# Fused threshold attention and MoE: head pairs on two row groups, DMA turns, MoE units in every attention step

## The chip, the cores and the metric

The kernel runs on one core of a Trainium2 chip. A core has TensorE (PE, matmuls into PSUM), VectorE (DVE), ScalarE (ACT), GpSimd (POOL) and SyncE (SP, which here only issues DMAs). The engines run side by side, each in the order of its own program, and wait for one another by semaphores. The metric is the device time of one execution in microseconds. Before the change the median of three runs is 1036.62 us (1034.22 to 1038.43).

## What is computed

There are 8 batches of 8 heads, 576 tokens and a head dimension of 64, all fp32. Attention keeps only the scores within tau = 0.02 of a row's maximum; the rest get weight zero. The heads are put side by side to 512 features per token, and two dense layers with a leaky ReLU between follow, for all 4608 tokens.

```python
scores = scale * np.matmul(q, k.transpose(0, 1, 3, 2))
thresh = np.max(scores, axis=-1, keepdims=True) - tau
scores = np.where(scores >= thresh, scores, -1000000000.0)
scores = scores - np.max(scores, axis=-1, keepdims=True)
attn = np.exp(scores)
attn = attn / (np.sum(attn, axis=-1, keepdims=True) + 1e-09)
attn_out = np.matmul(attn, v)
x = np.ascontiguousarray(attn_out.transpose(0, 2, 1, 3)).reshape(B * S, H * D)
h = x @ w_in                # 512 -> 2048
g = np.maximum(0.01 * h, h)
out = g @ w_out             # 2048 -> 512
```

## The kernel before

The Tile framework places buffers and semaphores; each engine's order comes from its scheduler, which may move work of different heads past each other. The loop at L272 runs over 65 iterations. Iteration `it` loads head it+4 (`head_loads`), prepares head it+2 (`prep`), computes the scores of head it (`stage_a_blk`), and finishes head it-1 (`rt_blk`, `pv_blk`, `pv_tail`). After every 16 heads `moe_group` runs the dense layers for two batches, 1152 tokens.

`prep`: GpSimd casts v to fp16 beside a column of ones (L93, L94). Nine PE transposes (L97) put q and k with the head dimension on partitions. ACT (L108) takes the fp16 high part, DVE (L109) the low part, so that a score is the sum of products of fp16 halves with nearly fp32 accuracy. Five DMAs of 72 KB (L113 to L117) place the halves.

`stage_a_blk`, for each of five blocks of query rows (four of 128 and one of 64): four matmuls over 128 rows (L137, L138) give 576 scores per query in PSUM; DVE takes the maximum (L139), GpSimd makes the bias of it (L142), and ACT writes relu(score - threshold) to `r` (L146). The weights are taken as 1 where `r` is positive; no exponential is computed.

`rt_blk`: 25 PE transposes per head turn `r` (L161), and DVE compares with zero while leaving PSUM (L167). `pv_blk`: 25 matmuls of 65 columns (L181), the last column giving the sum. `pv_tail`: DVE takes reciprocals (L196, L197), ACT scales (L201), five PE transposes turn the result (L207), and ACT copies it to the features-on-partitions tile `xTg` (L213).

`moe_group`: layer 1 in blocks of 512, 512 and 128 tokens (L238), with ACT (L245) and DVE (L249) sharing the leaky ReLU; layer 2 with 16 matmuls of 512 columns per 128 tokens (L257), a copy by ACT (L264), a 256 KB store (L265). All DMAs stand in SP's queue, the weights' too (L221, L226); GpSimd casts the weights (L222, L227).

PSUM holds two score tiles (`sc`, two banks each, also used for `qkt` and `ops`), two `rt` tiles (also used for `hps`), one `pv` and one `xt`.

Of the kernel before, what the change touches and what calls it, by code (L numbers as in the profile page):

```python
# [11 lines left out]
FP16 = mybir.dt.float16  # L12
AX = mybir.AluOpType
AF = mybir.ActivationFunctionType


@with_exitstack
def kernel(
# [10 lines left out]
    nc = tc.nc  # L29
    B, H, S, D = q.shape  # L30
    NH = B * H
    tau_f = float(tau)
    d_model = moe_w_in.shape[0]
    d_ff = moe_w_in.shape[1]
    SCALE = 1.0 / 8.0

    MT = [128, 128, 128, 128, 64]
    NQT = len(MT)
    NT9 = 9
    GB = 2  # L40
    NGRP = B // GB
    GTOK = GB * S

    sb = ctx.enter_context(tc.tile_pool(name="sb", bufs=1))
    ps = ctx.enter_context(tc.tile_pool(name="ps", bufs=2, space=bass.MemoryType.PSUM))

    I32 = sb.tile([128, 128], FP32, name="I32")
    make_identity(nc, I32)
    I16 = sb.tile([128, 128], FP16, name="I16")
    nc.gpsimd.tensor_copy(out=I16[:, :], in_=I32[:, :])  # L50

    BL0s = [sb.tile([128, 576], FP16, name=f"BL0_{i}") for i in range(3)]
    for t_ in BL0s:
        nc.gpsimd.memset(t_[64:128, 0:576], 0.0)
    def getBL0(h):
        return BL0s[h % 3]

    w_in16 = [sb.tile([128, d_ff], FP16, name=f"win16_{g}") for g in range(4)]
    w_out16 = [sb.tile([128, d_model], FP16, name=f"wout16_{j}") for j in range(16)]
    xTg = [sb.tile([128, GTOK], FP16, name=f"xTg_{g}") for g in range(4)]  # L60
    gT = [sb.tile([128, GTOK], FP16, name=f"gT_{j}") for j in range(16)]

    st = {}
    heads = {}

    def head_loads(h):
        b, hh = divmod(h, H)
        qk1 = sb.tile([128, NT9, 128], FP32, tag="qk1", bufs=4, name="qk1")
        v1 = sb.tile([128, NQT, 64], FP32, tag="v1", bufs=4, name="v1")
        vb = sb.tile([128, NQT, 65], FP16, tag="vb", bufs=6, name="vb")  # L70
        nc.sync.dma_start(
            out=qk1[0:64, 0:NT9, 0:64],
            in_=q[b, hh, :, :].rearrange("(t p) d -> p t d", p=64),
        )
        nc.sync.dma_start(
            out=qk1[0:64, 0:NT9, 64:128],
            in_=k[b, hh, :, :].rearrange("(t p) d -> p t d", p=64),
        )
        nc.sync.dma_start(
            out=v1[0:128, 0:4, 0:64],  # L80
# [186 lines left out]
    for h in range(4):  # L267
        head_loads(h)
# [62 lines left out]
```

## Time and profile before

| | |
|---|---|
| Median of three runs | 1036.62 us (1034.22 to 1038.43) |
| Span of the profiled execution, first to last instruction | 1038.0 us |
| Busy: PE / DVE / ACT / POOL | 910.3 / 517.5 / 492.9 / 123.4 us |
| Mean granted TensorE clock | 0.884 of full speed |
| DMA moved | 70.91 MB, 26.8% of 16 engines' span on the main queue |

The profile is one execution recorded by the hardware. A busy time is the time in which an engine had an instruction running; a matmul's duration includes its way through the array, so successive matmuls overlap and their rate is read from start times. A group of instructions is given by line, engine, operation, output<-input with shapes, count, then busy time and mean duration, then the idle time before them and what ended it. The clock row is in tenths of full speed. No duration is recorded for the execution apart from its span, so the span stands for it; it lies inside the range of the three runs.

### The profile page before, as it was taken

What the parts mean: (1) busy time and instruction counts of PE and PEld (TensorE: products, weight loads), DVE (VectorE), ACT (ScalarE), POOL (GpSimd) and SP (SyncE); (2) the same over time, 40 slices, a digit from 0 to 9 for tenths busy, and PEclk for the clock granted to TensorE, in tenths of its full rate; (3) what the DMA queues carried; (4) which work ended last, traced back from release to release, by engine and by line L of the source; (5) the groups of instructions that cost most, each with busy time, mean ns of one, the idle gap of its engine ahead of it and who ended that gap; (6) DMA issues with size and microseconds to landing.
All of it is one profiled execution on the core that took longest, in us unless ns stands there. A gap on an engine that the chain in (4) does not pass through costs nothing. (4 is left out here: it accounts for less than half of the span.)

```text
span 1038.0 us, 17867 instructions
## 1 busy us (share of the span) xinstructions
PE 910.3 (88%) x6720; PEld 515.5 (50%) x6720; DVE 517.5 (50%) x1024; ACT 492.9 (47%) x997; POOL 123.4 (12%) x606
## 2 busy tenths in 40 slices
PE   4999998897898998898898989898889989899888
PEld 2555555553345555553345555554335555554333
DVE  2644444654406566654424666665432666664440
ACT  2543334554425555554424555555432555554441
POOL 3221112110001111110000111111000111110000
PEclk9855556999999889989999888889999888987999
DMA  6823334340023333331013333332002333110002
GB/s 168 214 66 93 78 89 114 72 96 22 1 82 88 76 84 82 87 74 29 1 61 88 73 87 73 87 77 56 1 31 87 76 83 76 38 29 2 0 17 76
DMA packets 148438, 70.91 MB, mean 68 GB/s; under 512 B 120704, under 2 KB 141184, under 8 KB 147840
## 3 DMA queue, kind: packets, MB, share of 16 engines
q1 hardware_dynamic: 148352, 69.77, 26.8%
q8 instruction: 53, 0.87, 0.4%
q14 instruction: 33, 0.27, 0.1%
HBM read 36.70 MB, written 9.44 MB: 44 GB/s over the span
## 5 line engine op out<-in xcount | busy, mean ns | idle before, releaser
L146 ACT ACTIVATE r<-sc,bia 128x576 f16<-128x576 f32 (+1 forms) x320 | 234.3, 740 | 224.3 <-POOL bia L142 220.8
L139 DVE TENSOR_REDUCE mx<-sc 128x1 f32<-128x576 f32 (+1 forms) x320 | 238.0, 755 | 142.9 <-PE sc L138 138.7
L137 PE MATMUL sc<-BHH,QHL 128*128 128x512 f16 (+3 forms) x640 | 203.9, 331 | 40.5 <-ACT r L146 24.1
L161 PE MATMUL rt<-I_66,r 128*128 128x128 f16 (+3 forms) x1600 | 205.5, 240 | 7.9 <-DVE wT L167 6.9
L181 PE MATMUL pv<-vb,wT 128*128 128x65 f16 (+3 forms) x1600 | 150.4, 206 | 0.9 <-DVE wT L167 0.5
L167 DVE TENSOR_SCALAR wT<-rt 128x576 f16<-128x576 f16 (+1 forms) x320 | 134.5, 447 | 33.3 <-PE rt L161 33.1
L161 PEld LDWEIGHTS <-r 128*128 128x128 f16 (+3 forms) x1600 | 122.1, 108 | 58.3 <-issue 22.7
L245 ACT ACTIVATE hre<-hps 128x512 f32<-128x512 f32 (+1 forms) x192 | 93.8, 491 | 118.2 <-PE hps L238 118.2
L142 POOL TENSOR_SCALAR bia<-mx 128x1 f32<-128x1 f32 (+1 forms) x320 | 61.0, 191 | 695.9 <-DVE mx L139 651.3
L181 PEld LDWEIGHTS <-wT 128*128 128x128 f16 (+3 forms) x1600 | 98.5, 103 | 39.7 <-DVE wT L167 4.0
L138 PEld LDWEIGHTS <-QHL 128*128 128x128 f16 (+1 forms) x640 | 69.2, 112 | 85.8 <-issue 59.6
L137 PEld LDWEIGHTS <-QHL 128*128 128x128 f16 (+1 forms) x640 | 70.2, 111 | 73.4 <-issue 29.3
L238 PE MATMUL hps<-xTg_94,win_0_74 128*128 128x512 f16 (+1 forms) x192 | 62.8, 327 | 41.1 <-DVE gT_98 L249 5.4
L109 DVE SCALAR_TENSOR_TENSOR Al<-qkt,Ah 128x576 f16<-128x576 f32 x64 | 48.0, 750 | 93.3 <-ACT Ah L108 93.2
L108 ACT ACTIVATE Ah<-qkt 128x576 f16<-128x576 f32 x64 | 41.5, 649 | 81.9 <-PE qkt L97 81.6
L201 ACT ACTIVATE x<-pv,rcp 128x64 f16<-128x64 f32 (+1 forms) x320 | 70.3, 317 | 10.4 <-DVE rcp L197 10.4
L238 PE MATMUL hps<-xTg_97,win_3_77 128*128 128x512 f16 (+1 forms) x192 | 62.0, 326 | 2.4 <-ACT xTg_97 L213 2.4
L238 PE MATMUL hps<-xTg_95,win_1_75 128*128 128x512 f16 (+1 forms) x192 | 62.9, 327 | 0.0
L238 PE MATMUL hps<-xTg_96,win_2_76 128*128 128x512 f16 (+1 forms) x192 | 62.8, 328 | 0.0
L196 DVE RECIPROCAL rcp<-pv 128x4 f32<-128x4 f32 x64 | 11.7, 182 | 102.2 <-PE pv L181 98.2
L138 PE MATMUL sc<-BL_0_68,QHL 128*128 128x512 f16 (+1 forms) x220 | 60.7, 344 | 0.0
L264 ACT ACTIVATE osb<-ops 128x512 f32<-128x512 f32 x36 | 21.1, 596 | 81.7 <-PE ops L257 81.7
(350 smaller groups left out, 882.1 us busy)
## 6 DMA issues: line engine op xcount, KB each, us to landing
BHH<-Ah SPq DMA_DIRECT2D x128, 72.0 KB, 2.1
out_dram<-osb SPq DMA_DIRECT2D x36, 256.0 KB, 2.0
QHL<-Ah SPq DMA_DIRECT2D x64, 72.0 KB, 2.3
QHL<-Al SPq DMA_DIRECT2D x64, 72.0 KB, 2.0
wsti<-in_moe_w_in_dram SPq DMA_DIRECT2D x4, 1024.0 KB, 5.7
wsto<-in_moe_w_out_dram SPq DMA_DIRECT2D x16, 256.0 KB, 2.7
BL_0_68<-Al SPq DMA_DIRECT2D x22, 72.0 KB, 2.1
BL_1_69<-Al SPq DMA_DIRECT2D x21, 72.0 KB, 2.1
```

The source lines that it names most:

```text
L109: nc.vector.scalar_tensor_tensor(out=Al[0:128, 0:576], in0=qkt[0:128, 0:576], scalar=64.0, in1=Ah[0:128, 0:576], op0=AX.mult, op1=AX.subtract,
L137: nc.tensor.matmul(out=scp[0:M, ksl], lhsT=QHL[0:128, qs], rhs=BHH[0:128, ksl], start=True, stop=False, skip_group_check=True)
L138: nc.tensor.matmul(out=scp[0:M, ksl], lhsT=QHL[0:128, qs], rhs=BL0[0:128, ksl], start=False, stop=True, skip_group_check=True)
L139: nc.vector.tensor_reduce(out=mx[0:M, qt : qt + 1], in_=scp[0:M, 0:576], axis=mybir.AxisListType.X, op=AX.max,)
L142: nc.gpsimd.tensor_scalar(out=bia[0:M, qt : qt + 1], in0=mx[0:M, qt : qt + 1], scalar1=-RS * BS, scalar2=RS * (tau_f + 1e-9), op0=AX.mult, ...
L146: nc.scalar.activation(out=r[0:M, qt, 0:576], in_=scp[0:M, 0:576], func=AF.Relu, bias=bia[0:M, qt : qt + 1], scale=RS * BS,)
L161: nc.tensor.matmul(out=rt[0:Kc, ds(qt * 128, M)], lhsT=r[0:M, qt, ds(c * 128, Kc)], rhs=I16[0:M, 0:M], is_transpose=True, skip_group_check ...
L167: nc.vector.tensor_scalar(out=wT[0:Kc, c, 0:576], in0=rt[0:Kc, 0:576], scalar1=0.0, scalar2=None, op0=AX.is_gt,)
L181: nc.tensor.matmul(out=pv[0:M, qt, 0:65], lhsT=wT[0:Kc, c, ds(qt * 128, M)], rhs=vb[0:Kc, c, 0:65], start=(c == 0 and qt == 0), stop=(c == ...
L201: nc.scalar.activation(out=x[0:M, qt, 0:64], in_=pv[0:M, qt, 0:64], func=AF.Copy, bias=0.0, scale=rcp[0:M, qt : qt + 1],)
L238: nc.tensor.matmul(out=hps[0:128, 0:tb], lhsT=w_in16[gi][0:128, ts(j, 128)], rhs=xTg[gi][0:128, ds(co, tb)], start=(gi == 0), stop=(gi == ...
L245: nc.scalar.activation(out=hre[0:128, 0:tb], in_=hps[0:128, 0:tb], func=AF.Relu, bias=0.0, scale=0.99,)
```

## The change

Nearly the whole body is rewritten; the order of instructions on every engine is now the program's (`manual_schedule`).

A batch is 18 steps: 2 blocks x 4 head pairs x 2 halves of 128 query rows, then 2 tail steps for the last 64 query rows of all 8 heads. In a step the two heads of a pair lie on partitions 0 to 63 and 64 to 127, and their score matmuls (64 rows, 288 columns, three products of halves, two column blocks) alternate between the two (`scores`). The four score banks are all used by one step. DVE copies each head's scores to SBUF and takes the maximum in the same instruction (`copy_max`). In the next step `mask` makes a 16-bit integer of the distance from the threshold, and `weights` lets ACT compute an exponential, with the row sums as a by-product; in two steps of three one of the two heads is masked by ACT (Prelu with a slope of 1e20) instead of DVE.

A DMA that transposes turns the weights (`turn_w`, 128 x 1152 fp16), and pv follows four steps later (`PV_LAG`), v as the stationary operand, so that the result has d on partitions and needs no further turn. The two heads write PSUM partitions 0 to 63 and 64 to 127. The reciprocals of the sums are widened by GpSimd, turned by DMA (`turn_r`), and multiplied in by DVE when pv leaves PSUM (`evacuate`).

q and k are loaded as long rows, split into halves by GpSimd (by ACT and DVE for batch 0), and turned by DMA (`turn`, four turns of 64 x 1152 per load). `gate` makes each GpSimd operation wait for the last mask of DVE. The weights of the dense layers are cast by DMAs that GpSimd issues.

The dense layers are cut into units: `layer1` (512 PSUM columns, one Prelu by ACT) and `layer2` (two matmuls of 512 columns). The loop issues up to one of the first and two of the second in every step; what is left runs after step 144. Plain loads, turns and stores all stand in SP's queue, in the loop's order.

The removed lines are those printed above. The core of what takes their place:

```diff
--- before.py
+++ after.py
...
+PV_LAG = 4
...
+    ctx.enter_context(tc.manual_schedule())
...
+    UNIT = 64.0 * 64.0 * 8.0
+    NEAR = tau_f * UNIT
+    BIAS = -0.0625
...
+    def gate(inst, after):
+        if after is not None:
+            tc.add_manual_dep(inst.ins, after.ins.name,
+                              mybir.DependencyInfo(SYNC, ONLY_ORDER), reason="shared port")
+    def STEEP(st):
+        return st.n % 3 != 0
...
+    def load_qk(b, s, which, eng=None):
+        src = q if which == "q" else k
+        t = sb.tile([128, 2, 576], FP32, tag="raw", bufs=3, name="raw")
+        for c in range(2):
+            h0 = 4 * s + 2 * c
+            (eng or nc.sync).dma_start(
+                out=t[ds(64 * c, 64), :, :],
+                in_=src[b, ds(h0, 2), :, :].rearrange("h (p t) d -> p h (t d)", t=NT),
             )
+        raws[b, s, which] = t
...
+    def split_ops(b, s, which):
+        sc = 64.0
+        st = {}
+        def scale():
+            st["x"] = sb.tile([128, 2, 576], FP32, tag="scaled", bufs=1, name="scaled")
+            return nc.gpsimd.tensor_scalar(
+                out=st["x"][:, :, :], in0=raws[b, s, which][:, :, :], scalar1=sc, scalar2=1.0,
+                op0=AX.mult, op1=AX.mult)
+        def high():
+            st["h"] = sb.tile([128, NT, 2, 64], FP16, tag="half", bufs=4, name="half_h")
+            st["l"] = sb.tile([128, NT, 2, 64], FP16, tag="half", bufs=4, name="half_l")
+            halves[b, s, which] = (st["h"], st["l"])
+            return nc.gpsimd.tensor_copy(
+                out=st["h"][:, :, :, :].rearrange("p t h d -> p h t d"),
+                in_=st["x"][:, :, :].rearrange("p h (t d) -> p h t d", d=64))
+        def low(i):
+            return nc.gpsimd.tensor_tensor(
+                out=st["l"][:, :, i, :],
+                in0=st["x"][:, i, :].rearrange("p (t d) -> p t d", d=64),
+                in1=st["h"][:, :, i, :], op=AX.subtract)
+        return [scale, high, lambda: low(0), lambda: low(1)]
...
+    def turn(b, s, which):
+        res = []
+        for x in halves.pop((b, s, which)):
+            for c in range(2):
+                t = sb.tile([128, NT, 64], FP16, tag=f"{which}T", bufs=16, name=f"{which}T")
+                nc.sync.dma_start_transpose(
+                    out=t[:, :, :], in_=x[ds(64 * c, 64), :, :, :].rearrange("p t h d -> p (t h d)"))
+                res.append(t)
+        turned[b, s, which] = res
...
+    def cast_v(b, p, eng=None):
+        t = sb.tile([128, NT, 64], FP16, tag="v", bufs=10, name="v")
+        i = (eng or nc.gpsimd).tensor_copy(out=t[:, :, :], in_=vraws.pop((b, p))[:, :, :])
+        vs[b, p] = t
+        return i
...
+    def scores(st):
+        st.sc = [ps.tile([128, 2, 512], FP32, tag="sc", bufs=2, name=f"sc{h}") for h in range(2)]
+        for kh in range(2):
+            for i, (qh_, kh_) in enumerate(((0, 0), (1, 0), (0, 1))):
+                for u in range(2 if st.tail else 1):
+                    for h in range(2):
+                        pair = st.p + u
+                        if st.tail:
+                            lhs = cols(st, "q", h, qh_, pair, 512, 64)
+                            o = st.sc[h][ds(64 * u, 64), kh, 0:288]
+                        else:
+                            lhs = cols(st, "q", h, qh_, pair, 256 * st.blk + 128 * st.c, 128)
+                            o = st.sc[h][:, kh, 0:288]
+                        nc.tensor.matmul(out=o, lhsT=lhs, rhs=cols(st, "k", h, kh_, pair, 288 * kh, 288),
+                                         start=(i == 0), stop=(i == 2), skip_group_check=True)
+    def copy_max(st):
+        st.mx = sb.tile([128, 2], FP32, tag="mx", bufs=4, name="mx")
+        st.s = [sb.tile([128, 2, 288], FP32, tag=f"s{h}", bufs=2, name=f"s{h}") for h in range(2)]
+        for h in range(2):
+            nc.vector.tensor_scalar(
+                out=st.s[h][:, :, :], in0=st.sc[h][:, :, 0:288], scalar1=0.0, scalar2=None,
+                op0=AX.add, op1=AX.max, accum_out=st.mx[:, h : h + 1])
+    def mask(st):
+        st.steep = STEEP(st)
+        th = sb.tile([128, 2], FP32, tag="th", bufs=4, name="th")
+        if st.steep:
+            nc.vector.tensor_scalar(out=th[:, 0:1], in0=st.mx[:, 0:1], scalar1=0.5 - NEAR, scalar2=None, op0=AX.add)
+            nc.vector.tensor_scalar(out=th[:, 1:2], in0=st.mx[:, 1:2], scalar1=-1.0, scalar2=NEAR,
+                                    op0=AX.mult, op1=AX.add)
+        else:
+            nc.vector.tensor_scalar(out=th[:, :], in0=st.mx[:, :], scalar1=0.5 - NEAR, scalar2=None, op0=AX.add)
+        nh = 1 if st.steep else 2
+        st.y = sb.tile([128, 2, 576], INT16, tag="y", bufs=2, name="y")
+        for h in range(nh):
+            nc.vector.tensor_scalar(
+                out=st.y[:, h, :], in0=st.s[h][:, :, :].rearrange("p a b -> p (a b)"),
+                scalar1=th[:, h : h + 1], scalar2=-1.0, op0=AX.subtract, op1=AX.max)
+        i = nc.vector.tensor_scalar(
+            out=st.y[:, 0:nh, :], in0=st.y[:, 0:nh, :], scalar1=0x0400, scalar2=None, op0=AX.bitwise_xor)
+        st.th = th
+        return i
...
+    def weights(st):
+        key, j, n = quad(st)
+        if j == 0:
+            sums[key] = sb.tile([128, n, 2], FP32, tag=f"sum{n}", bufs=3, name="sum")
+        st.w = sb.tile([128, 2, 576], FP16, tag="w", bufs=3, name="w")
+        y16 = st.y[:, :, :].bitcast(FP16)
+        if st.steep:
+            st.z = sb.tile([128, 576], FP32, tag="z", bufs=1, name="z")
+        for h in range(2):
+            src, scale, bias = y16[:, h, :], 512.0, BIAS
+            if h == 1 and st.steep:
+                nc.scalar.activation(out=st.z[:, :], in_=st.s[1][:, :, :].rearrange("p a b -> p (a b)"),
+                                     func=AF.Prelu, bias=st.th[:, 1:2], scale=1.0, alpha=1e20)
+                src, scale, bias = st.z[:, :], 1.0 / UNIT, BIAS + 0.03125
+            nc.scalar.activation(out=st.w[:, h, :], in_=src, func=AF.Exp, bias=bias, scale=scale,
+                                 accum_out=sums[key][:, j, h : h + 1])
...
+        nc.sync.dma_start_transpose(out=wt[:, :, ds(128 * c, 128)],
+                                    in_=st.w[:, :, :].rearrange("p h k -> p (h k)"))
...
+    def widen(key, n):
+        wide[key] = sb.tile([128, n, 2, 64], FP16, tag=f"wide{n}", bufs=2, name="wide")
+        return nc.gpsimd.tensor_copy(
+            out=wide[key][:, :, :, :],
+            in_=recs.pop(key)[:, :, :].unsqueeze(3).to_broadcast([128, n, 2, 64]))
+    def turn_r(key, n):
+        rbs[key] = sb.tile([128, n, 128], FP16, tag=f"rb{n}", bufs=2, name="rb")
+        nc.sync.dma_start_transpose(out=rbs[key][:, :, :], in_=wide.pop(key)[:, :, :, :].rearrange("p n h d -> p (n h d)"))
...
+        for pair, o, cols in items:
+            vt = vs[st.b, pair]
+            for i in range(5):
+                for h in range(2):
+                    blk = i if h == 0 else 8 - i
+                    rows = ds(0, 128) if blk != 4 else ds(64 * h, 64)
+                    nc.tensor.matmul(out=o[ds(64 * h, 64)], lhsT=vt[rows, blk, :], rhs=wt[rows, blk, cols],
+                                     start=(i == 0), stop=(i == 4), skip_group_check=True)
...
+        nc.vector.tensor_tensor(out=o, in0=p_[:, :, :], in1=rin, op=AX.mult)
...
+    def layer1(deep=False):
+        g, u, nu = l1q.pop(0)
+        T = g.tokens
+        nj = 16 // nu
+        if u == 0:
+            g.g = sb.tile([128, 16, T], FP16, tag=f"g{T}", bufs=2, name="g")
+        hp = ps.tile([128, nj, T], FP32, tag="h", bufs=2, name="hp")
+        for jj in range(nj):
+            j = nj * u + jj
+            for i in range(4):
+                nc.tensor.matmul(out=hp[:, jj, :], lhsT=w_in16[:, i, ts(j, 128)], rhs=g.x[:, i, :],
+                                 start=(i == 0), stop=(i == 3), skip_group_check=True)
+        nc.scalar.activation(out=g.g[:, ds(nj * u, nj), :], in_=hp[:, :, :], func=AF.Prelu,
+                             bias=0.0, scale=1.0, alpha=0.01)
+        if u == nu - 1:
+            for m in range(T // 128):
+                for r in range(8):
+                    l2q.append((g, m, r))
+    pending_stores = []
+    def layer2():
+        g, m, r = l2q.pop(0)
+        if r == 0:
+            g.o = ps.tile([128, 512], FP32, tag="o", bufs=1, name="o")
+        for j in (2 * r, 2 * r + 1):
+            nc.tensor.matmul(out=g.o[:, :], lhsT=g.g[:, j, ts(m, 128)], rhs=w_out16[:, j, :],
+                             start=(j == 0), stop=(j == 15), skip_group_check=True)
+        if r == 7:
+            nm = g.tokens // 128
+            if m == 0:
+                g.osb = sb.tile([128, nm, 512], FP32, tag=f"osb{nm}", bufs=2, name="osb")
+            nc.scalar.activation(out=g.osb[:, m, :], in_=g.o[:, :], func=AF.Copy, bias=0.0, scale=1.0)
+            if m == nm - 1:
+                pending_stores.append(g)
...
+    for i in range(4):
+        nc.gpsimd.dma_start(out=w_in16[:, i, :], in_=moe_w_in[ts(i, 128), :])
+    for j in range(4):
+        nc.gpsimd.dma_start(
+            out=w_out16[:, ds(4 * j, 4), :],
+            in_=moe_w_out[ds(512 * j, 512), :].rearrange("(j p) f -> p j f", p=128))
...
+    while n < N + PV_LAG + 2 or l1q or l2q or pending_stores:
+        live = n < N
+        if live:
+            for f in loads_at.get(n, []):
+                f()
+            for f in turns_at.get(n, []):
+                f()
+            scores(steps[n])
+        if 1 <= n <= N:
+            last_mask = mask(steps[n - 1])
+        if n in rec_at:
+            recip(rec_at[n], quad_n := (2 if rec_at[n][1] == 2 else 4))
+        if n in ev_at:
+            evacuate(ev_at[n])
+        if live:
+            copy_max(steps[n])
+        if n in rec_at:
+            gate(widen(rec_at[n], quad_n), last_mask)
+        if live:
+            pool_work(n, last_mask)
+        if n in rb_at:
+            turn_r(rb_at[n], 2 if rb_at[n][1] == 2 else 4)
+        while pending_stores:
+            store()
+        if 1 <= n <= N:
+            weights(steps[n - 1])
+            turn_w(steps[n - 1])
+        has_pv = n in pv_at
+        if l1q:
+            layer1()
+        for _ in range(2):
+            if l2q:
+                layer2()
+        if has_pv:
+            pv(pv_at[n])
+        n += 1
...
```

## The prediction

> **What bounds the kernel now.** I read the page's busy shares and granted clock first, then the costliest groups, then windows by stage, then the instructions of single stretches in order of time.
>
> Page, busy shares and TensorE clock over 40 slices:
> ```profile
> PE 910.3 (88%) x6720; PEld 515.5 (50%) x6720; DVE 517.5 (50%) x1024; ACT 492.9 (47%) x997; POOL 123.4 (12%) x606
> ...
> PEclk9855556999999889989999888889999888987999
> ```
> TensorE is busy 88% and nothing else is above half. It also ran long stretches at half clock. Windows (span; busy of PE, PEld, DVE, ACT, POOL; clock; DMA share; GB/s), first MoE stages, then attention alone:
> ```profile
> 225.00:280.00 55.00, 44.68 (x262) 20.90 (x261) 26.96 (x53) 25.29 (x53) 2.17 (x11) 1.00 0.13 30
> 280.00:310.00 30.00, 28.80 (x141) 13.09 (x139) 3.64 (x7) 7.55 (x14) 0.00 (x0) 1.00 0.19 71
> ...
> 310.00:478.00 168.00, 149.40 (x1357) 94.26 (x1355) 104.39 (x210) 96.14 (x196) 25.64 (x144) 0.91 0.34 80
> ...
> 40.00:160.00 120.00, 111.39 (x707) 64.34 (x706) 54.89 (x109) 48.52 (x98) 24.35 (x87) 0.56 0.35 90
> ```
> In the MoE stages the other engines rest; in attention many small TensorE instructions set the pace. Groups of instructions, by form:
> ```profile
> L139 DVE TENSOR_REDUCE mx<-sc 128x1 f32<-128x576 f32 x256 | 190.0, 756 | 122.8 <-PE sc L138 121.8
> L146 ACT ACTIVATE r<-sc,bia 128x576 f16<-128x576 f32 x256 | 187.1, 741 | 208.7 <-POOL bia L142 208.6
> L161 PE MATMUL rt<-I_66,r 128*128 128x128 f16 x1024 | 133.3, 248 | 7.4 <-DVE wT L167 6.9 <-ACT r L146 0.3
> ...
> L167 DVE TENSOR_SCALAR wT<-rt 128x576 f16<-128x576 f16 x256 | 106.5, 449 | 32.5 <-PE rt L161 32.3
> ```
> The durations 756, 741 and 449 ns are the prices for what follows. TensorE's true rate is in the start times (start, duration), warm:
> ```profile
> 301.20 0.38 PE L257 MATMUL ops<-wout_6_84,gT_104 128*128 128x512 f16 x1
> 301.42 0.38 PE L257 MATMUL ops<-wout_7_85,gT_105 128*128 128x512 f16 x1
> ```
> ```profile
> 620.67 0.19 PE L137 MATMUL sc<-BHH,QHL 128*64 128x64 f16 x1
> 620.70 0.20 PE L138 MATMUL sc<-BL_0_68,QHL 128*64 128x64 f16 x1
> ```
> 512 columns pass in 0.216 us, 64 in 0.03; the rest of a duration, 0.16 us, is pass-through. SP's instructions:
> ```profile
> 17.51 0.58 SPq L221 DMA_DIRECT2D wsti<-in_moe_w_in_dram  x1
> 18.19 0.65 SPq L71 DMA_DIRECT2D qk_199<-in_q_dram  x1
> ```
> An issue takes 0.6 us for 144 KB and for 1 MB alike. DMA queues:
> ```profile
> q1 hardware_dynamic: 148352, 69.77, 26.8%
> ```
> 69.77 MB in 26.8% of 1038 us is 251 GB/s while moving.
>
> **The change, priced per step.** There are 144 steps (18 per batch: 16 of 128 query rows for two heads, 2 tail steps), each with about one layer-1 unit and two layer-2 units.
>
> *TensorE.* Removed per head: 9 transposes of q and k, 25 of r (0.08 us apart), 5 of x, and the 65-column matmuls. Kept: all MoE columns, 589,824 in total, 249 us at 0.216 per 512, so 1.73 per step. Scores: 12 matmuls of 288 columns with 64 rows, 1.46 us one after another, 0.73 if the two row groups run together. Weights times v: 10 matmuls of 256 columns per two steps, onto two column halves, 0.54 or 0.27 per step. No row shows two matmuls at once, so PE is 2.73 to 3.73. I take 2.73, because operands and outputs are disjoint halves; 3.73 stays for the range. Changing between row halves, the full array and column halves three times a step can cost nothing, or three pass-throughs, 0.48; I take 0.48. The clock in attention was 0.91, in MoE stages 1.00 even with PE busy 44.68 of 55 us; mixed, I take 0.93. PE: 2.73/0.93 + 0.48 = 3.4 us.
>
> [...]
>
> *VectorE.* Two copies with maximum from PSUM at 756: 1.51. Thresholds, 5/3 at 0.129 (the 64x1 reciprocal): 0.22. The int16 result from SBUF, 4/3 at 0.449 to 0.756, and the bitwise pass, 4/3 at 0.22 to 0.449: no row has these types; 16-bit work ran twice as fast per element, so I take 0.55 and 0.30, 1.13. The final multiply (36 of 692 ns) and reciprocals (40 of 182 ns) come to 0.22. Reading two accumulators, 0 to 0.129 each. Ends 2.85 and 3.8; I take 3.1 less some overlap (two reductions take 1.42, not 1.51): 3.0. Removed: the L167 and L249 passes.
>
> *ScalarE.* Two Exp and 2/3 Prelu at 741, one layer-1 Prelu of 512 (597), a quarter of the 596 ns copy: 2.72. The sums' read-out is 0 to 0.2 each (spacing of the 64-column copies at L201). I take 2.9. Exp is in no row; the toolchain lists Exp, Prelu and Copy in one table set, so I charge no reload.
>
> *GpSimd.* One split operation in 112 steps: 1152 elements by the 512-element cast of 611 ns and the 2048 one of 1.89 us are 1.14 us. Two inputs at 576, 0.66 to 1.3. It lies beside the 1.5 us of copies, for which the added wait on the last mask was placed; behind it queue v's casts and the widening, for which SP waits. Cost nothing; uncovered, 0.5 us in some 40 steps, 20 us. At the start GpSimd issues eight weight DMAs.
>
> *SP.* Per step 1.6 plain DMAs (8 q/k, 16 v, 5 stores per batch) at 0.6: 0.97. Turns: 39 per batch, 2.17 per step. Flat like the rows, 1.3; scaled by bytes from 72 KB, 3.7. SP 2.3 to 4.7; flat is nearer, since 1 MB took 0.58; I take 3.0. In order behind a turn that waits for Exp stand the next loads and stores.
>
> *DMA.* Turned: 295 KB of weights, 115 of q and k, 33 of reciprocals per step; plain 245. 687 KB at 251 GB/s are 2.7 us; with turns at half rate 4.5. I take 2.7, and pv comes three steps after its turn.
>
> [...] The flat rows give 545, and no run here shows a turn.
>
> *Sum.* PE leads with 3.4, the others are at 2.7 to 3.0 beside it. 144 x 3.4 = 490; the first 12 steps have no MoE work and go at VectorE's 3.0, -5. Ahead: load (up to 6 us with the weights underway), splits 3, eight turns 7 and landing 3, and SP's second eight turns before the first weight turn, in all 25. Behind: 18 steps of MoE alone at 1.73, the copy and a store's landing, 34. Together 544, so **545 us**, 0.52 of before. The profiled span is 1038.0, the median 1036.62, so span and time are taken as one.
>
> What is late next: the score banks are single, so scores wait for the copies of the step before, and the copies for the scores. PE has 2.0 us of MoE and pv in that gap and VectorE 1.2 of masks, so neither should lose more than 0.2.
>
> **Rivals.**
> 1. *The pairs do not run together* (the change does not do what it says). For: no overlap of two matmuls is seen in the trace, K=64 transposes at L97 included. PE 3.73 + 0.48 = 4.2 at full clock; 144 x 4.2 + 54 = 659.
> 2. *Turns bind.* For: none is in the trace, and 2.17 per step is much for one queue. Against: flat issue times. 4.5 per step gives 702 (by bytes 4.7, 731).
> 3. *Half clock.* For: 120 us at 0.56 while PE was busy 93%. Against: MoE stages held 1.00. 2 x 2.73 + 0.48 = 5.9; about 904.
> 4. *Slower.* Each turn waits for the one before to land. A 256 KB store landed 2.0 us after issue, a 256 KB load 2.7; 2.17 x (2.7 + 0.6) + 0.97 = 8.1 per step, 1220 us. It decides from (1037 - 54)/144 = 6.8 us per step. Against: copies of one queue overlap in the trace, five issues in 3.2 us with 2.1 to land.
>
> **How the numbers follow.** Forecast 0.52 (own range 455 to 610); pairs apart 0.17; turns bind 0.20; half clock 0.06; slower 0.04; about unchanged 0.01. The range takes the first two and two thirds of the third: 455 (VectorE's 2.85 less overlap, 2.75 x 144 + 59) to 740. All but the last two cases are faster: 0.95, same 0.01, slower 0.04, with 0.5% as the bound that a measurement can tell from no change.
>
> **What would show it.** Right: two score matmuls with starts a few ns apart in lines of the two heads; PE some 85% busy with the clock near 0.93; DVE and ACT above 80%; SP's turns at 0.6 to 1.0 us. Wrong: score matmuls 0.12 apart (rival 1); PE idle behind the wT turn, SP busy throughout (rival 2); clock at 0.5 (rival 3); one turn issued only at the landing of the last (rival 4).

## The result and the profile after

The changed kernel takes 731.65 us, the median of four runs (730.8 to 734.1). The kernel before took 1037.53 us (1034.22 to 1039.36) beside it. The ratio is 0.707, with a 95% interval of 0.704 to 0.710. The profiled execution has a span of 729.0 us and a mean granted clock of 0.894. Runs more than 1.5% above a kernel's fastest are left out of the medians and ratios here, but the profiles of experiments 6, 9 and 12 are of such runs (684.90, 662.02 and 644.43 us), so that their steps in the table are some 0.06 to 0.11 us too long. The forecast of 545 us missed by 187 us; the time lies in the range, at its upper end, where rival 2 (turns bind) stood.

The page of the changed kernel: busy times, clock and transfers over 40 slices, and the DMA queues (packets, MB, share of 16 engines' span).

```profile
PE 522.1 (72%) x4736; PEld 305.5 (42%) x4736; DVE 409.6 (56%) x1240; ACT 382.1 (52%) x861; POOL 183.7 (25%) x196
...
PEclk9999997798688988989879997999789997899999
DMA  9967887998798887999889877999889887887823
...
q1 hardware_dynamic: 320832, 102.68, 79.9%
q0 software_dynamic: 2688, 4.19, 3.1%
q10 hardware_dynamic: 576, 1.18, 0.8%
```

PE fell from 910.3 to 522.1 us and from 88% to 72% of a shorter span. No compute engine is busy throughout any more; the DMA row has mostly sevens to nines, where the kernel before had 26.8% on its main queue. All queues together (two small ones of 0.4 and 0.1% included) hold the 16 engines for 84.3% of 729.0 us. That is 614.5 us of full use for 108.89 MB, or 177 GB/s. The sum of the prediction used 251.

Windows of the changed kernel (span; busy of PE, PEld, DVE, ACT, POOL; clock; DMA share; GB/s): the first turns, then the middle, then the last batch, in which nothing is loaded or turned for a batch to come.

```profile
42.00:47.00 5.00, 1.98 (x12) 0.93 (x12) 4.89 (x13) 0.94 (x2) 0.00 (x0) 1.00 0.54 89
47.00:52.30 5.30, 3.32 (x23) 1.69 (x23) 4.72 (x17) 3.66 (x9) 0.00 (x0) 1.00 0.68 112
150.00:250.00 100.00, 78.26 (x693) 44.72 (x694) 61.59 (x190) 57.77 (x132) 31.25 (x31) 0.85 0.85 151
650.00:690.00 40.00, 40.00 (x401) 24.23 (x400) 35.22 (x110) 33.71 (x80) 2.06 (x4) 1.00 0.76 119
```

In the first two stretches nearly only q and k turns move: 89/0.54 and 112/0.68 are 165 GB/s at full use. In the last batch PE is busy 40.00 of 40 us. Measured from the first score copy of one step to that of the next, a step lasts 3.09 us there, and 4.65 on average in batches 1 to 6. So the compute engines could do what the sum said; in the middle something else takes some 1.6 us per step.

Groups of the changed kernel (line, engine, operation, output<-input, count; busy, mean ns; idle before and what ended it) that answer to the rows priced before:

```profile
L203 DVE TENSOR_SCALAR_CACHE_REDUCE s<-sc 128x576 f32<-128x576 f32 x288 | 205.6, 751 | 68.7 <-PE sc L196 68.0
L252 ACT ACTIVATE w<-y 128x576 f16<-128x576 f16 x192 | 130.2, 678 | 213.7 <-DVE y L225 168.1
...
L327 DVE TENSOR_TENSOR x<-pv,rb 128x512 f16<-128x512 f32 x32 | 22.1, 691 | 144.6 <-DMA rb<-wide 139.3
L222 DVE TENSOR_SCALAR y<-s,th 128x576 int16<-128x576 f32 x192 | 96.8, 525 | 1.7
...
L225 DVE TENSOR_SCALAR y<-y 128x1152 int16<-128x1152 int16 x144 | 53.2, 369 | 4.9
```

The durations are as priced. The large idle time is in the third line: DVE, about to multiply, waits 139.3 us in all for the turned reciprocals (`rb`).

The score matmuls and those of the weights with v, in order of time in the changed kernel (start, duration, how many run together in the line):

```profile
407.30 0.85 PE L305 MATMUL pv<-wT,v 128*64 128x256 f16 x10
408.08 0.91 PE L196 MATMUL sc<-kT,qT 64*128 64x288 f16 x12
```

In these stretches the two matmuls of a pair start 3 to 4 ns apart. The score pairs follow one another every 0.12 us, so twelve matmuls are six times that, 0.73 us, and the way through the array; the prediction had 0.73 for pairs that run together and 1.46 for pairs that do not. The pairs of the weights with v follow every 0.11 us (0.54 for the ten of two steps, 1.08 if they did not run together). Only the last of them, over 64 rows instead of 128, comes 0.20 after the one before it, and the scores 0.23 after that: a change of form costs some 0.1 us. The pairs run together, and rival 1 is out.

SP's instructions in one stretch of the changed kernel, in order of time:

```profile
379.03 3.60 SPq L268 DMA_TRANSPOSE wT<-w  x2
382.72 2.55 SPq L131 DMA_TRANSPOSE kT<-half_h  x2
385.36 2.55 SPq L131 DMA_TRANSPOSE kT<-half_l  x2
388.00 1.59 SPq L283 DMA_TRANSPOSE rb<-wide  x1
389.70 1.30 SPq L268 DMA_TRANSPOSE wT<-w  x1
391.05 1.25 SPq L78 DMA_DIRECT2D raw<-in_k_dram  x2
392.40 1.30 SPq L386 DMA_DIRECT2D out_dram<-osb  x2
```

SP goes from one issue to the next; a duration here includes SP's wait for its data, as in the first row. Without a wait a plain issue takes 0.6 us, a turn 1.3. SP's lines by source (smallest, median, largest ns):

```profile
L131 SPq DMA_TRANSPOSE kT<-half_l x32: 1221/1268/1457, 29.6 to 636.1; - x32
```
```profile
L268 SPq DMA_TRANSPOSE wT<-w x144: 1249/1325/3887, 65.9 to 691.5; - x144
```
```profile
L283 SPq DMA_TRANSPOSE rb<-wide x40: 1191/1217/2438, 83.0 to 694.3; - x40
```

147 KB, 295 KB and 131 KB cost 1.27, 1.33 and 1.22 us: a turn costs SP about twice a plain issue, nearly whatever its size. A batch has 16 x 1.27 + 18 x 1.33 + 5 x 1.22 for turns and 29 plain issues at some 0.67 (0.61 to 0.69), in all 70 us, 3.9 per step, of the 84 us that a batch of 4.65 us steps lasts.

The transfer engines come to nearly the same. A middle step moves 295 KB of weights, 131 of q and k and 33 of reciprocals turned, and 262 plain (loads of q and k 131, v 66, stores 65), 721 KB; at 177 GB/s that is 4.1 us. So there were two suspects, SP at 3.9 us and the engines at 4.1, and neither by itself explains 4.65.

### The profile page after: what moved, and what is told of

Its sections match the earlier page's. It is cut to its first block, busy times and chain, and to the rows that moved or that the text cites. A ratio compares the mean times of both kernels' runs of the same rounds, so it can differ in the third digit from the quotient of the medians.

```text
span 729.0 us, 13220 instructions
## 1 busy us (share of the span) xinstructions
PE 522.1 (72%) x4736; PEld 305.5 (42%) x4736; DVE 409.6 (56%) x1240; ACT 382.1 (52%) x861; POOL 183.7 (25%) x196
## 2 busy tenths in 40 slices
DMA packets 324161, 108.89 MB, mean 149 GB/s; under 512 B 308736, under 2 KB 310784, under 8 KB 324096
## 4 chain that ended last, share of the span: by engine, by line
PE 36%; DVE 17%; DMA 16%; SPq 15%; issue 8%; ACT 4%; POOL 4%; POOLq 0%; DVEq 0%; ACTq 0%
PE hp L353 11%; DMA rb<-wide 11%; SPq L131 10%; PE sc L196 10%; PE o L370 10%; DVE s L203 9%; PE pv L305 4%; DVE y L222 3%; SPq L148 3%; DMA raw<-in_q_dram 2%; POOL half_l L104 2%; DMA wT<-w 2%; ACT w L252 2%; DVE x L327 2%; DVE y L225 2%
## 5 line engine op out<-in xcount | busy, mean ns | idle before, releaser
L196 PE MATMUL sc<-kT,qT 64*128 64x288 f16 (+1 forms) x1920 | 167.1, 321 | 139.1 <-DVE s L203 103.8
L203 DVE TENSOR_SCALAR_CACHE_REDUCE s<-sc 128x576 f32<-128x576 f32 x288 | 205.6, 751 | 68.7 <-PE sc L196 68.0
L252 ACT ACTIVATE w<-y 128x576 f16<-128x576 f16 x192 | 130.2, 678 | 213.7 <-DVE y L225 168.1
L353 PE MATMUL hp<-x,win 128*128 128x256 f16 x1024 | 152.1, 296 | 41.5 <-DVE x L327 41.5
L196 PEld LDWEIGHTS <-qT 64*128 64x128 f16 (+1 forms) x1920 | 92.2, 106 | 201.2 <-issue 154.1
L370 PE MATMUL o<-wout,g 128*128 128x512 f16 x576 | 158.7, 402 | 1.3 <-ACT osb L376 1.3
L353 PEld LDWEIGHTS <-win 128*128 128x128 f16 x1280 | 113.7, 105 | 96.6 <-issue 78.9
L355 ACT ACTIVATE g<-hp 128x512 f16<-128x512 f32 x144 | 84.2, 584 | 78.4 <-PE hp L353 78.2
L327 DVE TENSOR_TENSOR x<-pv,rb 128x512 f16<-128x512 f32 x32 | 22.1, 691 | 144.6 <-DMA rb<-wide 139.3
L222 DVE TENSOR_SCALAR y<-s,th 128x576 int16<-128x576 f32 x192 | 96.8, 525 | 1.7
L305 PE MATMUL pv<-wT,v 128*64 128x256 f16 (+3 forms) x960 | 73.1, 269 | 20.5 <-DMA wT<-w 12.8
```

Of the source, the lines that this page charges most:

```text
L196: nc.tensor.matmul(out=o, lhsT=lhs, rhs=cols(st, "k", h, kh_, pair, 288 * kh, 288), start=(i == 0), stop=(i == 2), skip_group_check=True)
L203: nc.vector.tensor_scalar(out=st.s[h][:, :, :], in0=st.sc[h][:, :, 0:288], scalar1=0.0, scalar2=None, op0=AX.add, op1=AX.max, accum_out=st ...
L222: nc.vector.tensor_scalar(out=st.y[:, h, :], in0=st.s[h][:, :, :].rearrange("p a b -> p (a b)"), scalar1=th[:, h : h + 1], scalar2=-1.0, o ...
L252: nc.scalar.activation(out=st.w[:, h, :], in_=src, func=AF.Exp, bias=bias, scale=scale, accum_out=sums[key][:, j, h : h + 1])
L305: nc.tensor.matmul(out=o[ds(64 * h, 64)], lhsT=vt[rows, blk, :], rhs=wt[rows, blk, cols], start=(i == 0), stop=(i == 4), skip_group_check= ...
L353: nc.tensor.matmul(out=hp[:, jj, :], lhsT=w_in16[:, i, ts(j, 128)], rhs=g.x[:, i, :], start=(i == 0), stop=(i == 3), skip_group_check=True)
```

## Experiments

In all of them the step figure is the mean over batches 1 to 6, and "share" is the time of all queues' packets over 16 engines' span, as above. Packets of several queues overlap, so it can pass 100% (102.0% in 12).

| Kernel | us, median (range of all runs) | step, us | share |
|---|---|---|---|
| changed kernel | 731.65 (730.8 to 734.1) | 4.65 | 84.3% |
| 1 plain transfers off SP | 699.35 (699.01 to 710.95) | 4.44 | 92.0% |
| 2 k turned in one | 697.68 (695.53 to 699.50) | 4.39 | 88.3% |
| 3 weight turns of half the bytes | 701.97 (700.99 to 702.23) | 4.42 | 72.0% |
| 4 multiply a step later | 726.58 (724.75 to 727.99) | 4.54 | 85.1% |
| 5 reciprocals' turn first | 717.81 (715.32 to 724.04) | 4.51 | 85.4% |
| 6 = 1 and 5 | 675.76 (672.53 to 684.90) | 4.30 | 97.6% |
| 7 = 1, 5 and 3 | 609.25 (603.37 to 611.88) | 3.66 | 87.3% |
| 8 = 2, 5 and another start | 682.91 (677.59 to 683.47) | 4.27 | 88.2% |
| 9 = 1, 5 and 2 | 647.37 (646.76 to 662.02) | 4.11 | 101.6% |
| 10 no q, k turns after batch 0 | 588.84 (588.07 to 590.18) | 3.49 | 87.3% |
| 11 = 1, 5 and 10 | 571.45 (569.33 to 573.28) | 3.36 | 89.4% |
| 12 = 9, turns spread | 628.31 (628.31 to 646.24) | 3.99 | 102.0% |

Beside them the kernel before ran at 1028.7 (1 to 4), 1030.3 (5 to 8), 1029.3 (9 to 11) and 1028.4 us (12). For experiments 1 and 12 no interval of the ratio is on record; the figure for 12 is a single run.

**1. SP's plain issues taken away.** Loads of q, k and v go to GpSimd's queue (batch 0's q and k stay where they were), stores to ACT's; bytes are the same. The raw tile of v gets a fourth buffer.

```diff
-            (eng or nc.sync).dma_start(
+            (eng or nc.gpsimd).dma_start(
...
-                nc.sync.dma_start(
+                nc.gpsimd.dma_start(
...
-                nc.sync.dma_start(out=rows[:, bass.ds(t0 + h, 2, step=2), :], in_=g.osb[ds(64 * h, 64), :, :])
+                nc.scalar.dma_start(out=rows[:, bass.ds(t0 + h, 2, step=2), :], in_=g.osb[ds(64 * h, 64), :, :])
```

> All loads of q, k and v are issued from GpSimd and all stores from ScalarE; SP issues only turns. Bytes and turns are the same. Theory A (SP's issue time binds: 1.25 to 1.3 us per turn whatever its size, 0.66 per plain DMA, 70 us of SP work per batch of 84): SP's work falls to 51 us per batch, a step from 4.67 to 3.1-3.3 us, the time from 731.7 to 540-600 us. Theory B (the DMA engines bind: 687 KB per step at a share of 0.85 to 0.93): the same bytes, so 710-735 us. Theory C (VectorE blocked by the late reciprocal turn, nothing else): the turn still stands behind the q and k turns, so little, 680-720 us.

32 us came, against the 130 to 190 that SP alone would have given. The time lies in theory C's range, which 4 and 5 take up. SP now had more time to spare: its largest wait in this kernel (line waited for; us in all, times, longest) is

```profile
SPq L268 <- ACT w L252: 110.1, 43, 5.9
```

where the changed kernel had 67.1. But the transfer engines filled up. The queues' rows of this kernel:

```profile
q1 hardware_dynamic: 268608, 67.28, 64.1%
q0 software_dynamic: 12288, 30.16, 20.9%
q10 hardware_dynamic: 5824, 10.62, 6.5%
```

The first is SP's, now almost turns alone: 67.28 MB in 64.1% of 697.9 us are 150 GB/s of the packets' own time, where the plain transfers on the other two have 207 and 234. So turns are the slower kind, beside plain ones too. This kernel's windows, a middle stretch and one stall:

```profile
150.00:250.00 100.00, 79.65 (x710) 44.94 (x708) 63.61 (x194) 57.58 (x132) 54.78 (x69) 0.85 1.04 167
410.00:416.00 6.00, 1.42 (x14) 0.78 (x12) 0.00 (x0) 3.19 (x7) 1.72 (x2) 1.00 1.32 144
```

In the stall DVE does nothing for 6 us, while the engines' share is 1.32. SP alone is not the answer.

**2. Fewer turns, same bytes.** k is turned 128 rows at a time (1.36 to 1.40 us of SP for twice the bytes), so four turns per batch go; the score columns are cut 512 + 64, since the turned tile now interleaves two pairs.

```diff
+            if which == "k":
+                t = sb.tile([128, NT, 128], FP16, tag="kT", bufs=8, name="kT")
+                nc.sync.dma_start_transpose(
+                    out=t[:, :, :], in_=x[:, :, :, :].rearrange("p t h d -> p (t h d)"))
+                res.append(t)
+                continue
```

> The two turns of 64 x 1152 of each half of k become one of 128 x 1152: the same bytes in 4 turns fewer per batch; the score columns are cut 512 and 64 instead of 288 and 288. Theory A: 4 x 1.28 = 5 us per batch and 5 in the start, so 731.7 falls by 35-45 to 685-700 us, and the merged turn costs SP 1.3 us like the small one. Theory B: the same bytes, 725-735 us. Theory C: about half of A's gain.

The ratio to before is 0.678 (0.675 to 0.681): 34 us less than the changed kernel, with not a byte fewer, as theory A had it. SP's turns do cost time.

**3. Fewer bytes, same turns.** Only 640 of the 1152 columns of a step's weights are turned.

```diff
-        nc.sync.dma_start_transpose(out=wt[:, :, ds(128 * c, 128)],
-                                    in_=st.w[:, :, :].rearrange("p h k -> p (h k)"))
+        nc.sync.dma_start_transpose(out=wt[:, 0:5, ds(128 * c, 128)],
+                                    in_=st.w[:, :, :].rearrange("p h k -> p (h k)")[:, 0:640])
...
-                    blk = i if h == 0 else 8 - i
+                    blk = i
```

> Each weight turn moves 640 of 1152 columns (part of the weights is left out, and pv reads the same five blocks for both heads): as many turns, 131 KB fewer per step. Theory A: SP takes as long per turn, 720-735 us. Theory B: a fifth of the bytes is gone, 590-640 us. If SP's time per turn scales with blocks, a weight turn takes 0.7 us instead of 1.33 and the time falls by some 60-90 us.

0.682 (0.680 to 0.684), 30 us less, between the ranges of A and B. SP still paid 1.224 us per turn, so a turn's issue hardly follows its bytes. The main queue's row of this kernel (all queues: 72.0% of 700.2 us, 504.1 us):

```profile
q1 hardware_dynamic: 247104, 83.81, 67.5%
```

18.9 MB fewer took 614.5 - 504.1 = 110.4 us off the engines' packet time: weight turns run at 171 GB/s. Lowering either rate alone gives some 30 us, though 110 us of engine time went here, which suggests that each was covered by the other.

**4 and 5. The order alone.** Is the wait of the multiply for `rb` the loss itself? In 4 the multiply comes a step later; in 5 the reciprocals' turn is issued ahead of the q and k turns of the same step instead of behind them.

```diff
-    ev_at = {n + PV_LAG + 1: key for key, n in ends.items()}
-    pv_at = {s_.n + PV_LAG: s_ for s_ in steps if s_.tail or s_.c == 1}
+    ev_at = {n + PV_LAG + 2: key for key, n in ends.items()}
+    pv_at = {s_.n + PV_LAG + s_.tail: s_ for s_ in steps if s_.tail or s_.c == 1}
```

> The multiply with the turned reciprocals stands one step later in VectorE's order (and pv of the tail steps one step later). Theory A with SP at 70 us of 84 per batch: the part of the 14 us per batch in which SP waits for ScalarE comes back, at most 60-90 us, 640-700 us. Theory B: no change, 725-735 us. Theory C (VectorE waits 139 us for these turns): most of the 139 us, 590-640 us.

```diff
+            if n in rb_at:
+                turn_r(rb_at[n], 2 if rb_at[n][1] == 2 else 4)
             for f in turns_at.get(n, []):
                 f()
```

> Only the order in SP's queue changes: in a step that has both, the turn of the reciprocals is issued before the four turns of q or k. Theory O (the order makes the stalls: VectorE's multiply waits while four turns of 1.27 us, themselves waiting for GpSimd, stand ahead of the turn that it needs): the 6 to 13 us gaps at four steps of a batch shrink by about 5 us each and a step falls from 4.67 to SP's own 3.9-4.1 us, 635-660 us. Theory R (the rates alone: SP 3.9 us per step, the DMA engines 442 KB at the 165 GB/s that turns alone reached plus 245 KB at 251 GB/s, 3.66): the wait only moves to the weight turns, 700-730 us.

4 gave 5 us (0.706, 0.703 to 0.709), 5 gave 14 (0.699, 0.694 to 0.704), as theories B and R had it; theory C, with its 590 to 640, is out. The waits of the changed kernel, of 4 and of 5, on `rb` and on the weights' turn:

```profile
DVE x L327 <- DMA rb<-wide: 139.3, 27, 12.7
...
ACT w L252 <- DMA wT<-w: 45.4, 16, 16.2
```
```profile
ACT w L252 <- DMA wT<-w: 163.3, 46, 16.0
...
DVE x L327 <- DMA rb<-wide: 80.3, 26, 5.7
```
```profile
ACT w L252 <- DMA wT<-w: 202.1, 58, 15.7
...
DVE x L327 <- DMA rb<-wide: 78.3, 20, 8.1
```

What left the one wait turned up in the other: ACT can't write new weights because the tile it writes to is still being turned. The wait at the multiply showed where the queue was late, not why.

**6 and 7. Order and both rates together.** 6 is 1 and 5 in one kernel. 7 is 6 with the short weight turns of 3 besides, so it leaves out part of the weights as 3 does.

> e1_plain_off_sp with the order of e5. Theory O with both rates: SP needs 2.8, the DMA engines 3.66 us per step, so 3.7-3.9, and 705 falls to 600-630 us. Theory R: the DMA engines bind already in e1, 690-705 us. If GpSimd's new issues delay the widening, the gaps stay and it is above 660.

> e6 with the short weight turns of e3 (part of the weights is left out): SP 2.8 and the DMA engines 2.86 us per step, both below the 3.09 us that the last batch's steps take without loads. Theory O and R both say 3.1-3.4 us per step, 545-590 us; if it stays above 640, neither rate nor this order is the cause.

6: 0.657 (0.652 to 0.662), 7: 0.592 (0.587 to 0.596). 6 lies below R's range and above O's. It is also above 660, but not for the reason given for that: SP's waits for GpSimd come to 9 us in all in this kernel. From 6 to 7 the same cut in bytes that was worth 30 us in experiment 3 is worth 67. Once SP has room, bytes count. 7 ended above its 545 to 590: steps of 3.66 where 3.3 had been expected, and a start of 51.4 us to the first score copy.

**8. The start.** 2 and 5, and batch 0's loads all issued first (with a fourth buffer for them, and one fewer for v), the dense layers' weights held back behind the last split.

```diff
-        nc.gpsimd.dma_start(out=w_in16[:, i, :], in_=moe_w_in[ts(i, 128), :])
+        gate(nc.gpsimd.dma_start(out=w_in16[:, i, :], in_=moe_w_in[ts(i, 128), :]), last_split)
```

> e2's merged k turns, e5's order, and the start: all loads of batch 0 issued ahead of the splits and turns, the dense weights' DMAs behind the last split. Output as the reference's. SP 3.5, DMA 3.66 per step, the first score some 15 us earlier: theory O 590-630 us; theory R 670-690 us (the start alone).

0.663 (0.659 to 0.667), in theory R's range. The first score copy came at 23.7 us instead of 43.9, but then two steps of batch 0 stood for 19.8 and 15.7 us, and batch 0 ended at 124 us (23.7 + 18 x 5.58) instead of 128 in 2 and 5. The splits were done at 23.7, and the turns before took SP 1.2 to 1.8 us each; but the last k turn held it from 27.5 to 42.2 us, while the dense layers' weights, now issued from 24 us on (GpSimd had waited 23.6 us for the last split), were moving: 9.0 us from issue to landing in the median for `w_in`, 18.8 for `w_out`. SP then issued two loads of q, 16 of v and two of k before the first weight turn at 62.1. 2 and 5 without the new start were not run together, so what it gains by itself is not shown beyond batch 0. A start that is ready earlier gains little when the next thing on the same queue is not.

**9. All the cheap cures.** 1, 5 and 2 in one kernel; nothing is left out.

> This is the version with the plain transfers off SP and the reciprocals' turns ahead (677 us), with k turned four blocks at a time on 128 rows besides: four turns fewer in a batch, the same bytes. If SP's issue of turns still sets the steps there, 7 batches x 4 turns x 1.25 us go, 35 us: 637 to 650. If the transfer engines set them by bytes, which are unchanged: 665 to 680. A value between would say that a 128-row turn is also cheaper per byte on the transfer engines than a 64-row one.

0.630 (0.626 to 0.634), 28 us less than 6: in the range that stood for SP's issue of turns. The packets' time did not fall (671 us of engine time, 667 in 6), so 128-row turns are not cheaper for the engines; their share of the span rose from 97.6 to 101.6%. So a share of 98% in 6 did not mean that only bytes could help.

**10 and 11. The q and k turns taken away.** From batch 1 on batch 0's turned tiles are used again; in 10 in the changed kernel, in 11 in the kernel of 6. The scores of batches 1 to 7 are then of batch 0's q and k.

```diff
+        if b > 0:
+            halves.pop((b, s, which))
+            turned[b, s, which] = turned[0, s, which]
+            return
         res = []
```

> The changed kernel, but the turns of q and k are left out from batch 1 on and batch 0's turned tiles are used again (so the scores of batches 1 to 7 are of the wrong q and k; loads, splits and all arithmetic stay). SP's work per batch falls by 16 x 1.28 = 20.5 us (70 to 50 of the 84), the bytes of the turns by 28%: transfer engines 3.66 to about 2.96 us a step. If the excess of a step over the 3.1 us of the last batch comes from those two: steps of 3.3 to 3.6, 731 - 126 x 1.2 = 580, say 560 to 610. If only bytes matter, 0.70 us x 126 = 88 us go: 630 to 660. If the steps wait for the latency of the weights' own turn whatever else is there: 690 to 720.

> The same leaving out, in the version with the plain transfers off SP and the reciprocals' turns ahead (677 us). There SP has time to spare, so what goes is 115 KB a step of the transfer engines, 0.70 us at 165 GB/s: by bytes 677 - 126 x 0.70 = 589, no lower than 126 steps at 3.1 us allow (about 560): 560 to 605. If what is left in the 677 is not bytes but the order on the queue, less than half of it goes: 640 to 660. Against the changed kernel with the same turns left out it shows whether SP, once 20 us a batch lighter, still costs anything: within 15 us of each other if not.

10: 0.573 (0.570 to 0.575), 143 us less, as the sum of both rates had it. 11: 0.556 (0.553 to 0.559), 104 less than 6. SP, 20 us per batch lighter, still costs something: 17 us lie between the two, 0.13 us per step. The main queue's row of 10 (all queues: 87.3% of 588.4 us, 513.7 us):

```profile
q1 hardware_dynamic: 252736, 86.15, 81.8%
```

16.5 MB fewer took 614.5 - 513.7 = 100.8 us off the engines' time: q and k turns run at 164 GB/s, as the first windows said. In 11 a step moves 721 - 131 = 590 KB; at that kernel's 182 GB/s that is 3.24 us beside the 3.1 of computing, and it lasts 3.36.

**12. Is the burst to blame?** 9 with the next batch's q and k turns issued one per step, instead of four or two at once.

```diff
-            at(turns_at, base + 4 * i + 6, lambda b=b, s2=s2, w_=w_: turn(b, s2, w_))
+            for m, f in enumerate(turn_parts(b, s2, w_)):
+                at(turns_at, base + 4 * i + 6 + m, f)
```

> The 652.5 us version (plain transfers off SP, reciprocals' turns ahead, k turned on 128 rows) with the q and k turns of the next batch issued one a step (steps 6 to 9, 10 and 11, 14 to 17, 18 and 19) where they were issued four or two at once. Bytes and number are the same. If what is left of the stalls (steps of 8 to 15 us at the fours) comes of the burst itself, the weights' turn queued behind four others: most of the 20 to 25 us a batch above an even 3.3 us a step goes, 7 x 12 to 18, 530 to 575 by that; with half of it, 590 to 610. If the transfer engines have that much work to do whenever it is issued, spreading moves the waits about and gains little: 635 to 655. The first batch's start (50 us) is left as it is.

The lowest run is 19 us below the median of 9; the other three (638.67 to 646.24 us) lie about as far below the other two of 9 (657.07 and 662.02). No interval is on record, so the size of the gain is not certain. All four lie in or just below the 635 to 655 that stood for the engines' work, and above the 530 to 610 that stood for the burst. This kernel's DMA row and a middle window:

```profile
DMA  9998999999999999999997999999999999957812
```
```profile
150.00:300.00 150.00, 124.17 (x1192) 71.62 (x1194) 109.06 (x314) 93.45 (x219) 80.11 (x98) 0.91 1.13 178
```

The transfer engines are at 90% or more in nearly every slice up to the last batch. 178 GB/s is what the changed kernel moves at full use (177), and a step of 3.99 us is 721 KB at 181. This is the fastest version that leaves nothing out, 628.31 to 646.24 us, 85 to 103 us below the changed kernel.

**What they show together.** In 1, 6, 9 and 12 the bytes are those of the changed kernel, and the step goes 4.65, 4.44, 4.30, 4.11, 3.99, while the share goes 84, 92, 98, 102, 102%. The least that these bytes need is an estimate: the turns of a middle step at the 164 and 171 GB/s of 10 and 3, and its plain transfers at 195 (below) to 251 GB/s, are 3.8 to 4.1 us. 12 is there, and the step goes below it only when bytes go (7, 10, 11). The changed kernel lies some 0.6 to 0.8 us per step above because one in-order queue, itself occupied 3.9 us per step, does not keep the engines fed. That SP's cost and the engines' cost add in this way is argued from this sequence and from 2. The trace shows it only at the start, where turns whose data were ready took SP 2.9 to 4.8 us (and 14.7 in 8) while the dense layers' weights filled the engines. No run gave the weights more than three tiles (`w`) or moved pv of the full blocks later, so how much of the stalls a deeper pipeline would hide is open.

## Why the prediction was right and wrong

The span of 729.0 us is 184 over the sum's 544 or 545: the steps took 646 us (43.9 to 689.5) instead of 485, the start 43.9 instead of 25, the end 39.5 instead of 34. Even with the right terms the sum's rule, that the largest covers the rest, falls short: 126 steps at 4.1 us, 18 at the last batch's 3.09 and the measured start and end are 656 us. The other 73 us are, by this reckoning, overlap that did not take place. Point by point:

- **TensorE, right.** Score pairs and pv pairs run together, 0.73 and 0.27 us per step, as taken. The last batch needs 3.09 with PE busy throughout and the clock at 1.00. There each change of form (scores to layer 1, layer 2 to scores or to pv, pv from 128 to 64 rows and on to the scores) adds 0.09 to 0.12 us to the usual distance of two starts. With three changes per step on average that is 0.3, where 0.48, three pass-throughs of 0.16, was charged. The granted clock was 0.894 (taken: 0.93), and 0.96 to 0.98 in experiments 7, 10 and 11, where PE waits less (busy 88, 91 and 95% from 150 to 250 us, 78% in the changed kernel).
- **VectorE, ScalarE, right.** 409.6/144 = 2.84 us for 3.0, with 0.525 and 0.369 for the two unknown passes (taken: 0.55 and 0.30) and 0.083 for reading an accumulator. ScalarE: 2 x 0.68 + 2/3 x 0.76 + 0.58 + 0.15 + 2 x 0.187 = 2.97 for 2.9. It loaded its table once, 1.28 us at 11.8 us, ahead of the first split; Exp, Prelu and Copy ran without another, as charged. GpSimd, charged nothing, has 4% of the chain that ended last.
- **SP, wrong in size.** "flat is nearer" was right as a form: 1.22 to 1.40 us from 131 to 295 KB. But flat at the plain issue's 0.6 was wrong; a turn costs twice that. The term is 3.9, not 3.0.
- **DMA, the step that failed most.** "687 KB at 251 GB/s" priced turns by plain copies. Turns run at 164 to 171 GB/s. The 66 MB turned at that take some 395 us, and the other 43 MB have the remaining 220, 195 GB/s, so the plain transfers too were slower than in the kernel before. The bytes were also a mean over 144 steps, where a middle step has 721 KB. The term is 4.1, not 2.7. This was a bound that the working had in hand (4.5 with turns at half rate); it was passed over with "I take 2.7", with no row of a turn behind it.
- **Start, wrong.** 25 us covered everything before the first step; the first score copy came at 43.9 and the first weight turn at 65.9. The first q load landed after some 11 us, not 6. The first eight turns took 18 us (14.4 to 32.3), not 7: 8 x 1.27 are 10 of them. The splits were done at 16.6, but three turns issued between 17.0 and 29.5 took SP 2.9 to 4.8 us each, while the dense layers' weights were moving (until 29.6 us; the engines' share was 1.22 in that stretch). The working had the weights in the load's time alone. The second q load was issued only behind them, at 32.35.
- **Rival 2, right in name, by chance in number.** It had 4.5 to 4.7 per step, 702 to 731 us; measured were 4.65 and 731.65. But its 4.7 was SP's time by bytes, and SP's time did not go by bytes (1.22 us for 131 KB, 1.33 for 295). Two smaller costs, 3.9 and 4.1, made it together; that the number fits is luck. Rival 3 did not occur (clock 0.894), nor rival 4: SP goes on to the next turn after 1.3 us, while a weight turn lands 3.5 us after issue.

## What to carry to other kernels

Here a DMA that transposes cost its queue 1.22 to 1.40 us where a copy cost 0.6, and the engines moved it at 164 to 171 GB/s where plain transfers had 195 to 251. Price a turn's issue and its rate from a turn that has been measured, and where none has, let the forecast take the pessimistic end for a resource that gets 443 KB of new work every step. Add up every resource per step before choosing which binds; here two came out within 10%, neither cure alone paid 5%, and the experiments that told most were those that lowered both (7, 10). A long wait in the trace, like the 139.3 us for `rb`, named the instruction that stood last in a late queue; move it and see whether the wait goes or only changes its name.

## What was not expected of the hardware

- A turn's issue takes SP 1.22 to 1.40 us from 131 to 295 KB; a plain issue takes 0.61 and upward. While the dense layers' weights filled the engines (a share of 1.22 from 17.0 to 29.5 us), a turn whose data were ready held SP for up to 4.8 us, and for 14.7 in experiment 8.
- Turns within SBUF moved 164 (64 rows by 1152) to 171 GB/s (128 by 1152) at full use of the 16 engines, found both from the bytes taken away and, for the first, from windows with almost nothing else. Beside plain transfers on other queues they had 150 GB/s of their packets' time (experiment 1).
- Transfers from further queues share the engines with the first. With the plain ones off SP the packets' time for the same bytes grew from 614.5 us to 642 (experiment 1) and 667 (6), and the reciprocals' turn took 4.1 us from issue to landing in 1, where it had taken 2.5.
- A change between matmuls on row halves, the full array, column halves and 64 rows on column halves cost 0.09 to 0.12 us each in the last batch, at a clock of 1.00.
- From 150 to 250 us the granted clock was 0.85 in the changed kernel, with PE busy 78%, and 0.99 in experiment 11, with PE busy 95%. Gaps alone do not explain it: the kernel before had 0.56 from 40 to 160 us with PE busy 93%. What sets it was not tried.
